# Fourth block's chunk loads issued from GpSimd and sooner, with other PSUM banks, another order of ends, scalings and one last product in a fused retention and MLP kernel

## The chip, the cores and the metric

The kernel runs on one core of a Trainium2 chip. The metric is the device time of one execution in microseconds (us); lower is better. Runs of the kernel before spread from 612.08 to 613.63 us.

## The reference, cut to what matters

Two parts run one after the other: a retention recurrence over 4 batches, 8 heads, 768 tokens and 64 dimensions, and a two-layer MLP over the 3072 tokens that it gives.

```python
for t in range(S):                      # retention, S = 768
    state = gamma * state + einsum('bhd,bhe->bhde', k[:, :, t], v[:, :, t])
    y[:, :, t] = scale * einsum('bhd,bhde->bhe', q[:, :, t], state)
x = y.transpose(0, 2, 1, 3).reshape(3072, 512)
h = x @ w_in                            # 512 -> 2048
g = where(h > 0, h, exp(min(h, 0)) - 1) # ELU
out = g @ w_out                         # 2048 -> 512
```

## The kernel before, in words

**Tiling.** The tokens are cut into 24 chunks of 128 and six blocks of 512 tokens (four chunks each). Block 0 is computed plainly in its first layer; block 1 is computed alone; blocks 2 and 3, and then 4 and 5, are computed as two big blocks of 1024 tokens. Both layers use a seven-product scheme for 2x2 blocks (products numbered 1 to 7, taken in the order 1, 2, 6, 7, 5, 3, 4), nested twice in most stages. A product is a run of matmuls into one PSUM bank; what must be added to it is kept by ScalarE (ACT) copies and VectorE (DVE) sums.

**Order.** The order of instructions on every engine is written out by hand: generators yield at fixed places, and the loop around them calls the next piece of side work. Nothing is rescheduled. An engine runs its own list in order and waits for semaphores.

**PSUM banks.** `bank("a")` has two buffers, `bank("b")` and `bank("d")` one each; `ps_r` (tag "r") has four, shown as `x`, `sc`, `kv`, `y`.

**Retention side work.** For a block, `scores` (L331, masked at L342 on DVE), `states` (L371, summed at L383) and `outputs` (L427, L442) run between the matmuls of the layers. A chunk of q, k, v is one tile of 128x2048 numbers (1 MB) in a pool of four buffers, loaded by `load` (L125) on SP's queue. `scale_v` (L305) multiplies the chunk's v by powers of gamma before `states` may use it, on DVE when `by_vector` is true and on GpSimd (POOL) otherwise. The chunks 8 to 11 belong to block 2, the chunks 12 to 15 to block 3, which the title calls the fourth block.

**Stages that the change touches**, in order of time:

1. About 133 to 190 us: the first layer of block 1, `first(n)` for n = 0 to 3 (matmuls at L784, sums `h` at L731). Its loop loads the chunks 8 to 11, and at n = 3 runs `scores(2, ...)` and the four scalings of these chunks on DVE; then `states(2, ...)` follows.
2. About 183 to 241 us: the second layer of block 1, `second_twice(1, ...)`. Its weights come one product at a time from DRAM into the slots `wq` (L854, 256 KB each, eleven slots, refilled by `fetch` when a product is done), on SP's queue. There are 49 products of eight matmuls (L978). Its inner function `inner(j)` is called for j in `ORDER2 = [1, 2, 6, 7, 5, 3, 4]`. The loop around it loads and scales the chunks 12 to 15 at places of its steps: step n begins with `"first"` and has an `"end"`.
3. About 241 to 296 us: the first layer of the big block (L1279), with `scores(3, ...)` and the rest of block 3's retention.
4. About 296 to 334 us, and again at about 485 to 523 us: the layer of the big block that works with split weights (`passes`, L1342, and `big_rest`, L1329). For n = 0 to 7 it makes `six(n)` and `four(n)`, two sums of passes in PSUM; `six_sum` and `four_sum` (DVE, L918) rescale them and a third pass is added; `begin` (ACT, L1354 and L1355) and `end` (DVE, L1356) make the ELU of C11, C12, C21 and C22. C21 is read from `four`'s bank, C22 from `six`'s.
5. After each of these: the second layer of the big block (L1388), to the end.

The places of the loads and scalings of block 3, before:

```python
LOADS = {(1, "first"): 0, (2, "end"): 1, (4, "end"): 2, (5, "end"): 3}
...
if at in LOADS:
    load(3 * CPB + LOADS[at])
    scale_v(3 * CPB + LOADS[at])
```

Of the kernel before, what the change touches and what calls it, by code (L numbers as in the profile page):

```python
# [28 lines left out]
def kernel(  # L29
# [34 lines left out]
    nc = tc.nc  # L64
# [46 lines left out]
    chunks = [divmod(m, NCH) for m in range(NCHUNK)]  # L111
    raw = {}

    def load(m, cuts=(0, 2048), behind=None):

        if m >= NCHUNK:
            return
        t = ldpool.tile([P, 2048], FP32, name="chunk", tag="chunk")
        raw[m] = (
            t[:, 0:1024].rearrange("p (a h c) -> p a h c", a=2, c=C),  # L120
            t[:, 1024:2048].rearrange("p (a h d) -> p a h d", a=2, d=D),
        )
        hold(t, behind)
        for lo, hi in itertools.pairwise(cuts):
            nc.sync.dma_start(t[:, lo:hi], qkv[m, :, lo:hi])  # L125

    def hold(t, other):

# [697 lines left out]
    def want_second(tb):  # L826

        rest = []
        for j in BIG2 if tb > 1 else ORDER2:
            mine = []  # L830
            for k in (1, 2, 6, 7, 5) + ((4, 3) if j == 4 and tb == NTB - 1 else (3, 4)):
                if k in SMALL:
                    n = SMALL[k]
                    mine.append(((tb, j, k), scratch2[SEVEN[j]][:, 512 * n : 512 * n + 512]))
                else:
                    mine.append(((tb, j, k), scratch[4 * SLOT[j] + {1: 0, 2: 1, 4: 3}[k]].rearrange("p c -> p c")))
            for x in mine[:2] + rest + mine[2:5]:
                want(*x)
            rest = mine[5:]
        for x in rest:  # L840
            want(*x)
# [112 lines left out]
    def second_twice(tb, behind_last):  # L954
        quarter = lambda x, r, t: x[:, 4 * r : 4 * r + 4, P * t : P * t + P]
        ts, kept2 = {}, {}

        def inputs(j):
            for _ in input_parts(j):
                pass  # L960

        def input_parts(j):
            x = gq[INPUT2[j]]
            if j == ORDER2[-1]:
                t = w_all[:, :, 3072:3584].rearrange("p k (f d) -> p k f d", f=4)
            else:
                t = ts_[:, 2 * (len(ts) % 2) : 2 * (len(ts) % 2) + 2].rearrange("p n t -> p (n t)")
                t = t.rearrange("p (k f d) -> p k f d", k=4, f=4)
            b11, b12, b21, b22 = (quarter(x, a, b) for a in range(2) for b in range(2))
            for n, _ in enumerate(quarters_of_input(t, b11, b12, b21, b22)):  # L970
                if n == 1:
                    yield
            ts[j] = {1: b11, 2: b21, 3: b22, 4: t[:, 3], 5: t[:, 0], 6: t[:, 1], 7: t[:, 2]}

        def product(j, k, ps, begin):
            w = where[tb, j, k].rearrange("p (f d) -> p f d", f=4)
            for f in range(4):
                nc.tensor.matmul(  # L978
                    ps, lhsT=w[:, f, :], rhs=ts[j][k][:, f, :], start=(begin and f == 0), stop=(f == 3),
                    skip_group_check=True,  # L980
                )
            done((tb, j, k))

        def copy(ps):
            m = small.tile([P, P], FP32, name="ms", tag="ms")
            nc.scalar.copy(m, ps)
            return m

        def add(o, x, y):
            nc.vector.tensor_tensor(out=o, in0=x, in1=y, op=ALU.add)  # L990

        def inner(j):
            pool, tag = (mpool, "m") if j in (1, 6, 7, 5) else (hpool, "h")
            res = pool.tile([P, 2, 2, P], FP32, name="res", tag=tag)
            pa = bank("a")[:, 0, 0:P]
            product(j, 1, pa, True)
            m1 = copy(pa)
            pb = bank("b")[:, 0, 0:P]
            product(j, 2, pb, True)
            add(res[:, 0, 0], pb, m1)  # L1000
            yield
            product(j, 6, pa, False)
            u2 = copy(pa)
            pd = bank("d")[:, 0, 0:P]
            product(j, 7, pd, True)
            yield
            product(j, 5, pa, False)
            add(res[:, 1, 1], pd, copy(pa))
            yield
            product(j, 3, pa, False)  # L1010
            nc.scalar.copy(res[:, 0, 1], pa)
            yield
            product(j, 4, pd, False)
            add(res[:, 1, 0], pd, u2)
            sum_up(j, res.rearrange("p d t c -> p (d t c)"))

        def store(name, h):
            r, t = int(name[1]) - 1, int(name[2]) - 1
            nc.sync.dma_start(out[tb, r, t].rearrange("p d c -> p (d c)"), h)

        def sum_up(j, m):

            kept2[j] = m
            if j == 2:
                add(m, kept2[1], m)
                store("C11", m)
            elif j == 6:
                add(m, kept2[1], m)
            elif j == 5:
                add(m, kept2[6], m)  # L1030
                h = hpool.tile([P, 512], FP32, name="h", tag="h")
                add(h, m, kept2[7])
                store("C22", h)
                add(kept2[7], kept2[6], kept2[7])
            elif j == 3:
                add(m, kept2[5], m)
                store("C12", m)
            elif j == 4:
                add(m, kept2[7], m)
                store("C21", m)  # L1040

        for _ in input_parts(1):
            yield "input"
        yield "inputs"
        before = iter(())
        for at, j in enumerate(ORDER2):
            cur = inner(j)
            next(cur)
            if j == 1:
                yield "tail"  # L1050
            for _ in before:
                pass
            if at:
                yield "first"
            if j == 2:
                run(changes)
            if j == 7:
                changes = next_input(6)
            if j == 1:

                next(cur)
                yield "elu"
                next(cur)
            parts = input_parts(ORDER2[at + 1]) if at + 1 < 7 else iter(())
            if j in (2, 5, 3):

                next(parts)
            else:
                for _ in parts:
                    pass  # L1070
            if at == 6:
                behind_last()
            if j != 1:
                next(cur)
                yield "middle"
                next(cur)
            for _ in parts:
                pass
            if j == 1:
                flush()  # L1080
                changes = next_input(2)
                some(changes, 3)
            elif j in (7, 5):
                some(changes, 2)
            before = cur
            yield j
        for _ in before:
            yield "rest"
# [629 lines left out]
    for n in range(NQ):  # L1718
# [9 lines left out]
            next(cur)  # L1728
        if n == 3:
            next_part()  # L1730
        next(tail, None)
        next(cur)

# [5 lines left out]
            pass  # L1739
        if n == 3:  # L1740
            retention_step(2, 0)
            scale_v(2 * CPB, True)
        for at, s in enumerate(cur):
            next(sides[n], None)
            next(sides[n], None)
            if n and at >= (1, 2, 1)[n - 1]:
                next_part(n < 3)
            if at == 1 and n == 0:
                some(smalls[2], 2)
            elif at == 1 and n == 3:  # L1750
                for m in range(1, CPB):
                    scale_v(2 * CPB + m, True)
            if s == "gap":
                break
        for _ in sides[n]:
# [35 lines left out]
    flush()  # L1791
    retention_step(2, 2)
    step, VISITS = 0, {(1, "first"): 3, (1, "end"): 4}
    LOADS = {(1, "first"): 0, (2, "end"): 1, (4, "end"): 2, (5, "end"): 3}
    for s in sec:
        if s == "first":
            step += 1
# [7 lines left out]
        if at in VISITS:  # L1805
            retention_step(2, VISITS[at])
        if at in LOADS:
            load(3 * CPB + LOADS[at])
            scale_v(3 * CPB + LOADS[at])
        if at == (4, "end"):  # L1810
            scores(3, 0)
        elif at == (5, "end"):
# [11 lines left out]
    for nb in range(NB):  # L1824
# [3 lines left out]
        any_bank = lambda: ps_r.tile([P, 2, TH], FP32, name="x", tag="r")  # L1828

        def six(m):  # L1830
            q6[m] = any_bank() if m % 4 == 3 else bank("aba"[m % 4])
            passes(nb, m, 6, False, q6[m])

        def six_sum(m):
            stt(q6[m], q6[m], 4097.0, tile_of("C22" if m > 1 else "M1", m), ALU.add)

        def four(m):
            q4[m] = any_bank() if m % 2 else bank("d")
            passes(nb, m, 4, False, q4[m])

        def four_sum(m):
# [115 lines left out]
        for n in range(2 * NQ):  # L1957
# [23 lines left out]
                six_sum(n + 1)  # L1981
            if n == 0:
                end("C11", 2)
                end("C11", 3)
            elif n == 1:
                end("C21", 0)
                end("C11", 6)
            else:
                for x, m in (("C21", n - 1), ("C22", n - 2))[:: 1 if n % 2 else -1]:
                    end(x, m)  # L1990
            if n == 2:
                end("C11", 7)
            if n > 1:
# [108 lines left out]
```

## Time and profile before

| what | value |
|---|---|
| median of three runs | 612.93 us (612.08 to 613.63) |
| the profiled execution, its own time | 612.41 us |
| span of the profiled execution | 610.6 us |
| PE busy | 601.7 us (99%) |
| DVE busy | 507.6 us (83%) |
| ACT busy | 261.9 us (43%) |
| POOL busy | 96.8 us (16%) |
| granted TensorE clock | 1.00 |
| SP's DMA queue | 138.96 MB, 70.7% of 16 engines |
| mean DMA rate over the span | 229 GB/s |

The span is the time from the first to the last instruction on the chip; 1.8 us of the execution lie outside it. PE is TensorE's matmuls, PEld its weight loads, which overlap them. A busy PE is not a PE at its peak, since the ends of matmuls are modelled; so a lost stretch is read best from the distance of the starts of equal work. In the timeline a line gives start, length, engine, source line, operation, tiles, shapes and count, and in brackets the idle time before it and what ended it. In the chain of waits a line gives start, length and the piece of work that was last.

### The profile page before, as it was taken

Reading aid. Unit: us, or ns where it says so; the run is one execution under the profiler, and the core shown is the slowest. Engines: PE = TensorE matmul, PEld = TensorE weight load, DVE = VectorE, ACT = ScalarE, POOL = GpSimd, SP = SyncE. Lnnn points to the kernel's source line nnn. Section 1 sums busy time; section 2 is a strip of 40 time slices with the busy share of each in tenths; the row PEclk is TensorE's granted clock in tenths of the full one; section 3 lists DMA queues with packets and bytes.
Section 4 is the critical chain, followed back from the end, with each engine's and each line's share of the span. In section 5 each row is a group of like instructions: output and inputs, shape, how many; then the busy total and the mean of one; then the engine's idle time right before and its main releaser. Section 6 shows DMA issues by size and latency. Waiting matters only on the chain.

```text
span 610.6 us, 13757 instructions
## 1 busy us (share of the span) xinstructions
PE 601.7 (99%) x5510; PEld 493.7 (81%) x5510; DVE 507.6 (83%) x778; ACT 261.9 (43%) x448; POOL 96.8 (16%) x75
## 2 busy tenths in 40 slices
PE   8999999999999999999999999999999999999997
PEld 6765568888889998888766888888888866788886
DVE  6769889989789876889998877898658999778785
ACT  6889744205553112247688410010136779611110
POOL 2011000000220001000698000110000299000000
PEclk9999999999999999999999999999999999999999
DMA  8698578879977999588977445774555566556552
GB/s 307 283 384 310 169 221 265 239 240 263 355 241 232 297 344 345 181 293 277 365 246 224 120 129 157 268 279 122 183 165 162 168 216 183 168 154 186 153 152 114
DMA packets 85680, 139.85 MB, mean 229 GB/s; under 512 B 6896, under 2 KB 46576, under 8 KB 80880
## 3 DMA queue, kind: packets, MB, share of 16 engines
q1 hardware_dynamic: 85616, 138.96, 70.7%
q8 instruction: 44, 0.72, 0.5%
q14 instruction: 20, 0.16, 0.1%
HBM read 105.12 MB, written 33.82 MB: 228 GB/s over the span
## 4 chain that ended last, share of the span: by engine, by line
PE 90%; DMA 4%; DVE 2%; issue 1%; ACT 1%; SPq 1%; POOL 0%; ACTq 0%; DVEq 0%
PE pa L1388 16%; PE pa L1279 9%; PE pd L1388 8%; PE pd L1279 5%; PE pb L1388 4%; PE pa L557 3%; PE x L647 3%; PE pa L978 3%; PE pa L784 3%; DMA wq<-scratch_dram 3%; PE x L1342 3%; PE pb L1279 2%; PE pa L647 2%; PE y L427 2%; PE y L442 2%; PE pd L1342 2%
## 5 line engine op out<-in xcount | busy, mean ns | idle before, releaser
L1396 ACT COPY ms<-pa 128x256 f32<-128x256 f32 x41 | 15.2, 372 | 106.0 <-PE pa L1388 102.9
L1388 PE MATMUL pa<-gC,wq 128*128 128x256 f32 x240 | 56.8, 382 | 0.0
L1388 PEld LDWEIGHTS pa<-gC,wq 128*128 128x128 f32 x240 | 45.1, 190 | 7.2 <-issue 1.0
L305 POOL TENSOR_TENSOR chunk<-chunk,vf 128x512 f32<-128x512 f32 x15 | 18.7, 1256 | 166.0 <-DMA chunk<-in_qkv_dram 102.9
L1355 ACT ACTIVATE r<-r 128x512 f32<-128x512 f32 x64 | 40.4, 631 | 2.0
L1290 ACT COPY m<-pa 128x512 f32<-128x512 f32 x32 | 18.7, 584 | 36.5 <-PE pa L1279 32.2
L1400 DVE TENSOR_TENSOR res<-pd,ms 128x256 f32<-128x256 f32 x26 | 11.0, 422 | 28.0 <-PE pd L1388 17.5
L1388 PE MATMUL pd<-w_all,wq 128*128 128x256 f32 x120 | 28.4, 379 | 0.0
L1356 DVE SCALAR_TENSOR_TENSOR gC<-r,gC 128x512 f32<-128x512 f32 x24 | 28.1, 1178 | 0.0
L926 POOL TENSOR_TENSOR wp<-wp 128x512 fp32r<-128x512 f32 x6 | 8.4, 1400 | 116.4 <-DMA scratch_dram<-wi 102.7
L1388 PEld LDWEIGHTS pd<-w_all,wq 128*128 128x128 f32 x120 | 22.8, 190 | 3.1
L183 ACT ACTIVATE w_all<-wraw 128x1024 uint32<-128x1024 uint32 (+1 forms) x19 | 19.1, 1008 | 14.2 <-PE x L647 9.9
L1850 POOL TENSOR_TENSOR chunk<-chunk,w_all 128x512 f32<-128x512 f32 x4 | 5.1, 1286 | 126.2 <-ACT w_all L1290 126.2
L1370 DVE TENSOR_TENSOR gC<-w_all,gC 128x1024 f32<-128x1024 f32 x20 | 24.2, 1260 | 0.0
L1388 PE MATMUL pa<-ts,wq 128*128 128x256 f32 x96 | 22.9, 381 | 0.0
L1388 PE MATMUL pa<-w_all,wq 128*128 128x256 f32 x96 | 22.9, 381 | 0.0
L185 ACT ACTIVATE w_all<-wraw 128x1024 fp8e4<-128x1024 f32 (+1 forms) x19 | 22.6, 1189 | 0.6
L1388 PE MATMUL pd<-ts,wq 128*128 128x256 f32 x96 | 22.7, 379 | 0.0
L557 PE MATMUL pa<-xb,w_all 128*128 128x512 f32 x48 | 21.5, 597 | 0.0
L1422 ACT COPY res<-pa 128x256 f32<-128x256 f32 x13 | 4.8, 372 | 38.1 <-PE pa L1388 38.1
L213 DVE CUSTOM_DVE_ANT_0 w_all<-wraw,w_all 128x2048 uint16<-128x2048 uint16 (+1 forms) x19 | 20.1, 1057 | 0.8
L514 ACT ACTIVATE r<-r 128x512 f32<-128x512 f32 x32 | 20.2, 630 | 1.0
(361 smaller groups left out, 1605.5 us busy)
## 6 DMA issues: line engine op xcount, KB each, us to landing
wq<-scratch_dram SPq DMA_DIRECT2D x231, 256.0 KB, 3.4
chunk<-in_qkv_dram SPq DMA_DIRECT2D x22, 1024.0 KB, 7.2
wraw<-in_w_dram SPq DMA_DIRECT2D x15, 1024.0 KB, 6.2
scratch_dram<-wp SPq DMA_DIRECT2D x8, 512.0 KB, 4.4
out_dram<-res SPq DMA_DIRECT2D x7, 512.0 KB, 3.4
scratch_dram<-gT SPq DMA_DIRECT2D x12, 256.0 KB, 4.4
wq<-scratch_dram SPq DMA_DIRECT2D x24, 128.0 KB, 3.2
scratch_dram<-w_all SPq DMA_DIRECT2D x12, 256.0 KB, 3.1
```

Of the source, the lines that this page charges most:

```text
L183: nc.scalar.activation(flat, lo, AF.Copy, scale=2.0**-29)
L185: nc.scalar.activation(top, hi.bitcast(FP32), AF.Copy, scale=2.0**-120, saturate=False)
L213: vec.tensor_tensor(out=flat, in0=c, in1=flat, op=ALU.add)
L514: nc.scalar.activation(e, e, AF.Exp, scale=-1.0)
L557: nc.tensor.matmul(hp, lhsT=w[n][:, fi, j // 2, j % 2, :], rhs=xb[:, j, :], start=(j == 0), stop=(j == 3))
L647: nc.tensor.matmul(X[j][:, d, :], lhsT=w[j][:, d * P : d * P + P], rhs=x[j], start=(n == 0 and d == 0), stop=at_end, skip_group_check=True,)
L1279: nc.tensor.matmul(ps[:, f, :], lhsT=w[:, f, :], rhs=big_xs[j][k], start=(begin and f == 0), stop=True, skip_group_check=True,)
L1342: nc.tensor.matmul(joined(ps), lhsT=where[name][:, c : c + P].bitcast(F32R), rhs=x[:, k], start=(not third and c == 0), stop=(k == 1), ski ...
L1355: nc.scalar.activation(r, r, AF.Exp, scale=-1.0)
L1356: return lambda: nc.vector.scalar_tensor_tensor(g, r, -1.0, h, ALU.add, ALU.max)
L1370: nc.vector.tensor_tensor(out=quarter(to, r, t), in0=quarter(x, r, t), in1=quarter(y, r, t), op=op)
L1388: nc.tensor.matmul(ps, lhsT=w[:, f, :], rhs=ts[j][k][:, f // 2, f % 2, :], start=(begin and f == 0), stop=(f == 3), skip_group_check=True,)
```

## The change

- `load` takes a queue. The loads of the chunks 12 to 15 are issued from GpSimd's queue, at earlier places: (1, "first"), (2, "first"), (3, "end") and (4, "end"). The scaling of a chunk is called one place later than its load, also on GpSimd.
- The four scalings of the chunks 8 to 11 on DVE are called earlier: two within n = 2 of `first`, two at the beginning of n = 3, ahead of the scores.
- In the last `inner(j)` of the second layer of block 1 (j = 4), product 4 comes before product 3, into a bank `b` of its own; its summand u2 takes up `pd` first. The order in which the weights of these two are fetched changes with it.
- In stage 4, `six` uses the banks a, b, a, d in turn (before a, b, a, r), and `four` always one of the four r buffers (before d for even n, r for odd n).
- In stage 4 the ends of C22 and C21 always come in this order (before, in turns), and the end of C11's tile 3 comes one step later.

```diff
-    def load(m, cuts=(0, 2048), behind=None):
+    def load(m, cuts=(0, 2048), behind=None, queue=nc.sync):
...
-            nc.sync.dma_start(t[:, lo:hi], qkv[m, :, lo:hi])
+            queue.dma_start(t[:, lo:hi], qkv[m, :, lo:hi])
...
-            for k in (1, 2, 6, 7, 5) + ((4, 3) if j == 4 and tb == NTB - 1 else (3, 4)):
+            for k in (1, 2, 6, 7, 5) + ((4, 3) if j == 4 and tb in (1, NTB - 1) else (3, 4)):
...
+            if j == ORDER2[-1]:
+                pb = bank("b")[:, 0, 0:P]
+                product(j, 4, pb, True)
+                add(u2, pd, u2)
+                add(res[:, 1, 0], pb, u2)
+                yield
             product(j, 3, pa, False)
             nc.scalar.copy(res[:, 0, 1], pa)
-            yield
-            product(j, 4, pd, False)
-            add(res[:, 1, 0], pd, u2)
+            if j != ORDER2[-1]:
+                yield
+                product(j, 4, pd, False)
+                add(res[:, 1, 0], pd, u2)
...
         if n == 3:
             next_part()
+            for m in range(2, CPB):
+                scale_v(2 * CPB + m, True)
...
             retention_step(2, 0)
-            scale_v(2 * CPB, True)
...
-            elif at == 1 and n == 3:
-                for m in range(1, CPB):
-                    scale_v(2 * CPB + m, True)
+            elif at and n == 2:
+                scale_v(2 * CPB + at - 1, True)
...
-    LOADS = {(1, "first"): 0, (2, "end"): 1, (4, "end"): 2, (5, "end"): 3}
+    LOADS = {(1, "first"): 0, (2, "first"): 1, (3, "end"): 2, (4, "end"): 3, (5, "end"): 4}
...
-            load(3 * CPB + LOADS[at])
-            scale_v(3 * CPB + LOADS[at])
+            n = LOADS[at]
+            if n < CPB:
+                load(3 * CPB + n, queue=nc.gpsimd)
+            if n:
+                scale_v(3 * CPB + n - 1)
...
-            q6[m] = any_bank() if m % 4 == 3 else bank("aba"[m % 4])
+            q6[m] = bank("abad"[m % 4])
...
-            q4[m] = any_bank() if m % 2 else bank("d")
+            q4[m] = any_bank()
...
             if n == 0:
                 end("C11", 2)
-                end("C11", 3)
             elif n == 1:
                 end("C21", 0)
+                end("C11", 3)
                 end("C11", 6)
             else:
-                for x, m in (("C21", n - 1), ("C22", n - 2))[:: 1 if n % 2 else -1]:
-                    end(x, m)
+                end("C22", n - 2)
+                end("C21", n - 1)
```

## The prediction

> **What bounds the kernel now.** I read the page first: busy times, then the slices.
>
> ```profile
> PE 601.7 (99%) x5510; PEld 493.7 (81%) x5510; DVE 507.6 (83%) x778; ACT 261.9 (43%) x448; POOL 96.8 (16%) x75
> PE   8999999999999999999999999999999999999997
> DMA  8698578879977999588977445774555566556552
> ```
>
> PE is the bound from end to end and leaves 8.9 us of its span. Nothing that the change does takes matmuls away, so it can only win places where PE stands, and lose by making new ones. Where it stands is read from the chain of waits. In the second layer of block 1 (window 176 to 262 us):
>
> ```profile
> 210.83 9.84 DMA wq<-scratch_dram
> 220.67 0.14 issue
> 220.81 1.13 PE pd L978 x8
> ...
> 238.00 0.02 issue
> 238.02 0.28 ACT ms L986
> 238.29 0.04 issue
> 238.34 1.16 PE pa L978 x8
> 239.50 0.89 PE pd L978 x8
> ```
>
> PE stood for weights that were under way for 9.84 us, and later for a copy on ACT. An undisturbed product is 0.89. In the layer with split weights the chain and the timeline (PE, DVE) show the period of one step, as the distance of the starts of L1329:
>
> ```profile
> 303.19 1.88 PE L1329 MATMUL pa<-xb,w_all 128*128 128x512 f32 x4
> 308.31 1.88 PE L1329 MATMUL pb<-xb,w_all 128*128 128x512 f32 x4
> 312.81 1.88 PE L1329 MATMUL pa<-xb,w_all 128*128 128x512 f32 x4
> ...
> 301.51 2.97 DVE L1356 SCALAR_TENSOR_TENSOR gC<-r,gC 128x512 f32<-128x512 f32 x2
> 304.41 0.69 DVE L918 SCALAR_TENSOR_TENSOR x<-x,m 128x512 f32<-128x512 f32 x1
> ...
> 314.97 0.69 DVE L1356 SCALAR_TENSOR_TENSOR w_all<-r,pd 128x512 f32<-128x512 f32 x1 [0.17 <-ACT r L1355]
> 315.73 0.30 PEld L1342 LDWEIGHTS pd<-xr,wq 128*128 128x128 f32 x2 [0.54 <-PE pa L1342]
> ```
>
> The periods are 5.12, 4.50, then (next starts 317.68, 322.19, 326.66) 4.87, 4.51, 4.47, with the same work in each. So two steps lose 0.62 and 0.38.
>
> **Scalings of block 2.** Timeline, 180 to 190 us:
>
> ```profile
> 179.98 2.48 DVE L305 TENSOR_TENSOR chunk<-chunk,vf 128x512 f32<-128x512 f32 x4
> 180.80 2.40 PE L371 MATMUL kv<-chunk 64*64 64x64 f32 x112
> 188.92 0.68 DVE L731 TENSOR_TENSOR h<-pd,m 128x512 f32<-128x512 f32 x1
> 189.66 0.97 PEld L978 LDWEIGHTS pd<-ts,wq 128*128 128x128 f32 x8 [0.33 <-DVE h L731]
> ```
>
> The `kv` matmuls go at the pace of the scalings (the chain has 2.01 for such a run at 357.25, here 2.33 to the next product at 183.13) and begin 0.1 late; and DVE's list is so long afterwards that `h` frees `pd` late: the product before starts at 188.47, so 189.36 was due and 189.66 came. That is 0.3 + 0.1 + 0.3 = 0.7 us. The change puts the four L305 (0.62 each, 2.5 in all) among DVE's gaps at 166.07 to 167.10, 168.39 to 169.36 and 173.89 to 174.48, which sum to 2.6; the chunks landed by 164.6. The later two stand ahead of ELU sums, which come up to 0.7 later; the next one that PE needs, `h` at 175.09 to 175.77, has until 177.14. So I take -0.7, from 0 to -0.7.
>
> **Product 4 before product 3.** In between ACT copies `pa`, so the wait at 238.34 is covered by 0.89 of matmuls. Lost before: start to start 236.93 to 238.34 is 1.41 against 0.89, and the product after the stop takes 0.99 instead of 0.89. I take -0.6. DVE gets one 128x128 add more (0.28) before the last, and bank `b` must be read before the next stage's second product, two products later, which is cover of some 1.7 us; without it 0.3 comes back. Range 0 to -0.6.
>
> **Banks and ends of the split-weight layer.** The first loss is `four_sum(1)` behind two ends of C11 on DVE (2.97 us; they take 1.49 each here beside GpSimd's work, 0.68 elsewhere). With one of them moved a step later, the sum starts when ACT's copy is done at 303.07, about 1.4 earlier, and PE needs it 0.62 earlier. The moved end falls in a step in which DVE then runs ahead by as much. The second loss is a matmul that wants bank `d` while the end of C21 reads it (until 315.65). With the four r buffers the reader has three steps more. `six(7)` in `d` needs the end of C22(3), which now comes first in its step, two steps before. The bank changes of `six` hold four steps apart, as before. So both losses go: -1.0, in each of two layers (the second has 5.15 and 4.90 at the same steps): -2.0. Range 0 to -2.0; DVE is busy for nearly all of this stage, so that half of it could reappear one step on.
>
> **The loads.** Off SP's list go four issues (0.4 each), which hold up nothing. What counts is when the bytes move. GpSimd's list is then: load 12, load 13, scale 12, load 14, scale 13, load 15, scale 14, scale 15. It is not paced by PE's steps, only by free buffers and landings: chunk 8's buffer is free at 197.7 (the wait that SP shows for its load), the other three when `outputs` is through at 202.3. So load 12 leaves at 197.7, load 13 at 202.4, load 14 behind scale 12 near 206, load 15 near 210, where they left at 197.7, 209.6, 224.0 and 236.4. An issue from GpSimd has no row here: SP's takes 0.4, GpSimd's own work on a chunk 1.3; either lies in GpSimd's idle time and moves these starts by 1 us at most.
>
> All four megabytes thus fall ahead of the weights that PE waited for at 220.67 (the 32nd product's), where two did. There is little slack for them:
>
> ```profile
> core 0: us, PE busy (x) PEld busy (x) DVE busy (x) ACT busy (x) POOL busy (x), PEclk, DMA share, GB/s
> 198.00:213.00 15.00, 15.00 (x225) 14.74 (x215) 12.40 (x27) 2.12 (x8) 1.04 (x1) 1.00 0.91 299
> 213.00:222.00 9.00, 8.16 (x72) 7.84 (x71) 6.98 (x13) 1.33 (x5) 1.14 (x1) 1.00 1.00 375
> ```
>
> Only 9% of 15 us is idle. By landings: in a backlog a 256 KB transfer follows the one before by 0.65 (206.25, 206.89, 207.55); a chunk adds 2.5 (215.33 to 217.84, 229.17 to 231.69) to 4.1 (201.62 to 205.63, 239.22 to 243.31), 3.28 in the mean. After the landing at 201.62 there stand twelve weights, one output store of the same size and four chunks: 201.62 + 13 x 0.65 + 4 x 3.28 = 223.2. PE wants these weights at 217.78 + 2 x 0.89 = 219.56, so it stands 3.6, plus 0.14 from landing to start. What it lost before goes: starts 217.78, 218.97, 220.81 instead of steps of 0.89, 1.25 us. Net +2.5; with 2.5 a chunk -0.6, with 4.1 +5.8. Some of it may show a few products earlier, not more of it. Later the weights have no chunk beside them, but none was late there.
>
> **Sum.** -0.7 - 0.6 - 2.0 + 2.5 = -0.8. The profiled execution took 612.41 (span 610.6 and 1.8 around it), giving 611.6; it lies 0.5 under the median of the runs, 612.93, from which I forecast 612.1. A change of about 0.3% (1.84 us) is what a measurement of this kernel can tell from none.
>
> **Rivals.** *B, the weights keep their pace.* Two queues share the DMA engines, and the sum above lets the chunks go first. If the two share evenly while both have work, weights land every 1.3 instead of 0.65: the 32nd by 201.62 + 13 x 1.3 = 218.5, before 219.56. Then no stall is left: -3.3 - 1.25 = -4.55, 608.4. For it: chunks are not needed before the scores at 222.8. Against it: a row of a chunk is 8 KB, of a weight 2 KB, so that turns row by row would give the chunk four fifths; no run shows two queues so far. [...]
>
> *C, slower: the chunks take the long price.* At 4.1 a chunk the stall is 7.1 at about 212 to 220 us, net +5.8, and with the gains +2.5: 615.4. It eats the gains from 3.5 a chunk on, and is slower than the bound from 3.9 on. For it: the two chunks that took 4.1 did so with the engines over 0.9 busy; against it, the two that took 2.5 stood in a full queue, as these will.
>
> *D, GpSimd's issues hold DVE.* Ends beside GpSimd's work take 1.34 in the mean against 0.68; were each of the four issues and shifted scalings to cost PE 0.66, it is +2.6 on the forecast, 614.7. Against it: GpSimd's four scalings ran here before without a stop of PE behind them. [...]
>
> **How the numbers follow.** Forecast 0.36, B 0.30, C 0.24, D 0.10. Faster by over 0.3%: B, and the forecast where a chunk adds under 3.0 (0.06): 0.36. Slower: C but for 0.02, D for 0.07, and 0.03 of the forecast where the layer's gain fails: 0.32. Within: 0.32. The forecast's own range is 610.5 to 614.3. With B and C in, 608.2 to 615.8.
>
> **What would show it.** In the profile after: periods of 4.5 at all L1329; no wait of `pa L978` for `ms L986` near 238; `kv` in 2.0 near 180. A wait for `wq` of 2 to 4 us between 210 and 222 is the forecast, none is B, over 5 is C. GpSimd's DMA lines show the issue's length, and DVE sums over 0.7 beside them would be D. The forecast is wrong if load 14 or 15 leaves after 215, or if new waits stand in the split-weight layer.

## The result and the profile after

The changed kernel takes 615.76 us in the median (613.11 to 617.17), the kernel before 612.55 in the runs beside it (610.21 to 614.13). The ratio is 1.0052, 95% interval 1.0034 to 1.007: slower by 3.2 us (2.1 to 4.3). Forecast were 612.1, a gain of 0.8 us, and a chance of 0.32 for slower by over 0.3%. The time lies outside the forecast's own range (610.5 to 614.3). It is just inside the wider one (to 615.8) because that range takes in rival C, and C's mechanism is not what the runs show; so this is luck.

The profiled execution of the changed kernel took 617.17 us (span 615.4), one of its long ones. Its page, beside the lines shown of before:

```profile
PE 603.3 (98%) x5510; PEld 494.0 (80%) x5510; DVE 510.4 (83%) x779; ACT 261.8 (43%) x448; POOL 99.3 (16%) x79
PE   8999999999999899999999999999999999999997
DMA  8698578789977998498976345784555576556552
```

PE leaves 12.1 us of its span where it left 8.9, and one slice has fallen to 8: the fourteenth, from 200 to 215 us. The waits of PE (us in total, times, longest) say for what:

```profile
PE pd L978 <- DMA wq<-scratch_dram: 2.0, 1, 2.0
...
PE x L1349 <- DVE x L918: 1.1, 4, 0.4
PE x L1349 <- DMA wq<-scratch_dram: 0.7, 1, 0.7
...
PE pa L978 <- DMA wq<-scratch_dram: 0.5, 1, 0.5
PE pd L1395 <- PE pa L1395: 0.5, 2, 0.3
PE pb L978 <- DMA wq<-scratch_dram: 0.4, 1, 0.4
```

The same list of the kernel before has for this layer:

```profile
PE pd L978 <- DMA wq<-scratch_dram: 0.7, 1, 0.7
...
PE pa L978 <- ACT ms L986: 0.4, 1, 0.4
```

In the second layer of block 1 (L978) the waits for weights are 2.9 us, where before they were 0.7; the split-weight layer (now L1349) waits four times for `four_sum` (L918) and once for a weight; and a new wait, of `pd` at L1395, stands behind each split-weight layer. The two gains that were forecast ahead of them are there. Timeline (PE and DVE) from 165 to 190 us, and the chain of waits:

```profile
165.89 0.68 DVE L305 TENSOR_TENSOR chunk<-chunk,vf 128x512 f32<-128x512 f32 x1
...
168.19 0.69 DVE L305 TENSOR_TENSOR chunk<-chunk,vf 128x512 f32<-128x512 f32 x1
...
170.48 2.35 DVE L305 TENSOR_TENSOR chunk<-chunk,vf 128x512 f32<-128x512 f32 x2
...
180.57 2.08 PE L371 MATMUL kv<-chunk 64*64 64x64 f32 x112
182.58 1.16 PE L978 MATMUL pa<-gC,wq 128*128 128x128 f32 x8
...
188.87 1.16 PE L978 MATMUL pd<-ts,wq 128*128 128x128 f32 x8
```

```profile
207.69 12.69 DMA wq<-scratch_dram
220.38 0.04 issue
220.42 1.16 PE pb L978 x8
...
237.56 0.89 PE pd L978 x8
238.45 0.89 PE pa L978 x8
239.34 0.89 PE pd L978 x8
```

The scalings run 9 to 14 us earlier and `kv` to the next product takes 2.01 instead of 2.33; near 238 every product follows in 0.89, with no stop for ACT's copy. But a weight that was asked for at 207.69 lands 12.69 us later, and PE stands 0.4 for it. The longest stop, of 2.0, comes before that, for a weight that was asked for at 201.18 and landed at 213.02.

To see where the time went, I cut six profiled executions at the same instructions (us; each is one execution, so that a difference under about 0.5 may be chance):

| stretch | before | changed | changed, second profile | loads only | banks and ends only | best |
|---|---|---|---|---|---|---|
| first L784 of block 1 to first L978 | 49.74 | 49.30 | 49.31 | 49.73 | 50.30 | 49.30 |
| from there to the first L1279 | 57.10 | 60.17 | 60.06 | 60.43 | 56.38 | 55.40 |
| to the first L1329 | 62.96 | 63.16 | 66.10 | 62.16 | 62.64 | 62.32 |
| to the first L1388 | 30.94 | 32.03 | 30.64 | 30.89 | 30.73 | 30.70 |
| to the last matmul | 273.04 | 273.61 | 273.66 | 273.00 | 273.64 | 272.66 |

(Lines by the numbers of before.) The second row, the layer that shares the DMA engines with the loads, carries the loss in both profiles of the changed kernel. The second of them has 3.1 us more in the third row, which come back below.

### The profile page after: what moved, and what is told of

Its sections match the earlier page's. It is cut to its first block, busy times and chain, and to the rows that moved or that the text cites. A ratio compares the mean times of both kernels' runs of the same rounds, so it can differ in the third digit from the quotient of the medians.

```text
span 615.4 us, 13748 instructions
## 1 busy us (share of the span) xinstructions
PE 603.3 (98%) x5510; PEld 494.0 (80%) x5510; DVE 510.4 (83%) x779; ACT 261.8 (43%) x448; POOL 99.3 (16%) x79
## 3 DMA queue, kind: packets, MB, share of 16 engines
q0 software_dynamic: 576, 4.19, 1.8%
## 4 chain that ended last, share of the span: by engine, by line
PE 91%; DMA 5%; DVE 2%; issue 1%; ACT 1%; DVEq 0%; SPq 0%
PE pa L1395 16%; PE pa L1286 9%; PE pd L1395 8%; DMA wq<-scratch_dram 5%; PE pa L784 5%; PE pd L1286 4%; PE pb L1395 4%; PE pa L557 3%; PE x L647 3%; PE x L1349 3%; PE pa L978 3%; PE pb L1286 2%; PE pd L784 2%; PE pa L647 2%; PE kv L371 2%; PE y L427 2%
## 5 line engine op out<-in xcount | busy, mean ns | idle before, releaser
L1395 PE MATMUL pa<-gC,wq 128*128 128x256 f32 x240 | 56.8, 381 | 0.0
L1395 PEld LDWEIGHTS pa<-gC,wq 128*128 128x128 f32 x240 | 45.1, 190 | 7.3 <-issue 1.0
L1362 ACT ACTIVATE r<-r 128x512 f32<-128x512 f32 x64 | 40.4, 631 | 2.0
L1363 DVE SCALAR_TENSOR_TENSOR gC<-r,gC 128x512 f32<-128x512 f32 x24 | 29.8, 1246 | 0.0
L1395 PE MATMUL pd<-w_all,wq 128*128 128x256 f32 x120 | 28.5, 380 | 0.5 <-PE pa L1395 0.5
L1395 PEld LDWEIGHTS pd<-w_all,wq 128*128 128x128 f32 x120 | 22.6, 190 | 4.2 <-issue 1.2
L1349 PE MATMUL x<-xl,wq 128*128 128x512 f32 x64 | 23.6, 454 | 1.1 <-DVE x L918 1.1
L1395 PE MATMUL pa<-ts,wq 128*128 128x256 f32 x96 | 22.9, 381 | 0.0
L1395 PE MATMUL pa<-w_all,wq 128*128 128x256 f32 x96 | 22.9, 381 | 0.0
L1395 PE MATMUL pd<-ts,wq 128*128 128x256 f32 x96 | 22.7, 379 | 0.0
L986 ACT COPY ms<-pa 128x128 f32<-128x128 f32 x21 | 5.6, 266 | 36.7 <-PE pa L978 35.2
```

The lines of the kernel that those rows point to most:

```text
L1349: nc.tensor.matmul(joined(ps), lhsT=where[name][:, c : c + P].bitcast(F32R), rhs=x[:, k], start=(not third and c == 0), stop=(k == 1), ski ...
L1362: nc.scalar.activation(r, r, AF.Exp, scale=-1.0)
L1363: return lambda: nc.vector.scalar_tensor_tensor(g, r, -1.0, h, ALU.add, ALU.max)
L1395: nc.tensor.matmul(ps, lhsT=w[:, f, :], rhs=ts[j][k][:, f // 2, f % 2, :], start=(begin and f == 0), stop=(f == 3), skip_group_check=True,)
```

## The experiments

Theory: the loss is the loads' (**L**), because four chunks overtake the weights. Rival: it is the split-weight layer's (**S**), whose banks and ends shift the wait to other steps. Ratios are against the kernel before, run beside; the us in brackets are the interval times 612.4.

**Each part alone, and all but the loads.** The edits are the hunks of the change taken apart: `e_loads_only` has the queue, LOADS and late `scale_v`; `e_layer_only` these:

```diff
-            q6[m] = any_bank() if m % 4 == 3 else bank("aba"[m % 4])
+            q6[m] = bank("abad"[m % 4])
-            q4[m] = any_bank() if m % 2 else bank("d")
+            q4[m] = any_bank()
...
+                end("C11", 3)      # at n == 1, no more at n == 0
...
+                end("C22", n - 2)
+                end("C21", n - 1)
```

`e_scale_m4` has the early scalings and product 4 before 3; `e_no_loads` is the changed kernel without the hunks of `e_loads_only`.

> Theory L (the loads cost the time): the four megabytes ahead of the weights make PE stand three times between 213 and 221 us as in the profile of the changed kernel (2.2, 0.7 and 0.6 us there), and this part alone is slower than the kernel before by 2.5 to 4.0 us. Rival S (the split-weight layer costs the time, and the loads only seem to, since the stops are made good later): this part alone is within 1 us of the kernel before. The recorded sum has +2.5 for it.

> Theory S (the new banks and ends themselves put four_sum late in other steps): the first split-weight layer loses about 1.5 to 2 us again, with waits of a third pass for x L918, and this part alone is 0.5 to 2 us slower. Rival S' (the loss of 2.1 us seen in the first of these layers came with its place in time, after the loads, or with a late load of weights near 303 us): the banks and ends alone gain 0.4 in each of the two layers and pay 0.4 after each for the bank d of six(7), so that this part is within 0.5 us, or gains as recorded, up to -2.0.

> Both theories: the earlier scalings take 0.7 us out of the stretch from 133 to 190 us and the exchange of products 4 and 3 takes 0.6 us out of 236 to 241 us, as the trace of the changed kernel has them, so that this part alone is 1.3 us faster (0.21%), if no later wait takes it back; a rival in which DVE's list or a late load takes it back has it within 0.5 us.

> Everything of the change but the loads. Theory L: all that the loads cost is gone, -1.3 for scalings and products and between -0.8 and +0.8 for the split-weight layer: 0.5 to 2 us faster than the kernel before, 4 us faster than the changed kernel. Theory S: still slower than before by 0.5 to 2 us.

| kernel | median us | ratio, 95% interval | us |
|---|---|---|---|
| loads only | 615.96 | 1.0052 (1.0031 to 1.0073) | +3.2 (1.9 to 4.5) |
| banks and ends only | 612.30 | 0.9999 (0.998 to 1.0018) | -0.1 (-1.2 to 1.1) |
| scalings and product 4 | 610.82 | 0.997 (0.9955 to 0.9985) | -1.8 (-2.8 to -0.9) |
| all but the loads | 611.29 | 0.9988 (0.9968 to 1.0008) | -0.7 (-2.0 to 0.5) |

The loads alone cost as much as the whole change, and without them it is not slower: L holds, and S does not carry the loss alone. The waits of PE of the kernel with the loads only are of the same kind, in the same layer:

```profile
PE pb L978 <- DMA wq<-scratch_dram: 1.9, 1, 1.9
PE pa L978 <- DMA wq<-scratch_dram: 1.8, 2, 1.5
```

**How many chunks go ahead.** (Products are counted from 0 in the expectations: product 31 is the prediction's 32nd.) Only the loads are changed; the chunks 14 and 15 (then only 15) go back to SP's queue and their old places:

```diff
+            n = LOADS[at]
+            if n < 2:                                    # e_three_early: n < 3
+                load(3 * CPB + n, queue=nc.gpsimd)
+            elif n > 2:                                  # e_three_early: n > 3
+                load(3 * CPB + n - 1)
+            if n:
+                scale_v(3 * CPB + n - 1)
```

> The kernel before, with only the chunks 12 and 13 from GpSimd's queue and sooner; 14 and 15 stay on SP's queue at their old places. Theory of the bytes ahead (the loss is the lateness of the first weight behind the last chunk that overtakes; landings 201.62 + n x 0.65 + chunks x 3.28): product 27, due at 216.0, would have its weights at 201.62 + 9 x 0.65 + 2 x 3.28 = 214.0 and product 31, due at 219.6, at 216.6, so no stop is left in this layer and the 1.2 us of the kernel before go too: 1.2 us faster. Rival, the queue itself (any load from GpSimd beside SP's costs the weights about 0.9 us a chunk): 1.8 us slower.

> The same with the chunks 12, 13 and 14 from GpSimd's queue and sooner, 15 on SP's queue at its old place. Theory of the bytes ahead: product 27 at 217.3 against 216.0, so that 1.4 us are lost and 1.2 are won: within 0.7 us of the kernel before. Rival, the queue itself: about 2.7 us slower. If the cost grows by the same amount with each chunk, both are wrong.

Two early: 611.09, ratio 0.999 (0.9971 to 1.001), -0.6 us (-1.8 to 0.6). Three early: 613.4, 1.0023 (1.0007 to 1.0039), +1.4 us (0.4 to 2.4). Four early, above: +3.2. The rival, a price of each load from GpSimd's queue, had 1.8 and 2.7 for the first two; both lie outside. The theory had 1.2 won for two and "within 0.7" for three; the first lies inside the interval, and of the second the interval covers only its upper end. In the profile with two, no product of this layer waits for a weight, and the stretch takes 56.08 us against 57.10; with three the waits are 0.5 and 0.2; with four 1.5, 1.9 and 0.3. So what counts is what lies ahead in the queues, beyond a point. The gain of 1.2 forecast for two was not seen in full in the median: the stop that it removes is not in every execution of the kernel before (below).

**The size of the rows.** The four loads as in the change, each in four pieces:

```diff
-                load(3 * CPB + n, queue=nc.gpsimd)
+                load(3 * CPB + n, (0, 512, 1024, 1536, 2048), queue=nc.gpsimd)
```

> The loads as in the changed kernel (four from GpSimd's queue, sooner), but each in four pieces of 512 columns, so that a row is 2 KB as a row of the weights is; nothing else is changed against the kernel before. If the engines go from queue to queue row by row (in the profile of the changed kernel the two queues show about as many packets of 8 KB as of 2 KB in a stretch, 82 and 86 from 211 to 213 us), the chunk's share falls from four fifths to a half, weights land every 1.3 us, the 27th by 213.3 and the 31st by 218.5, and the stops go: up to 1.2 us faster. If only the bytes count, it costs 3 to 4 us as before. Three GpSimd issues more for each chunk, of unknown length, may take some of it back.

617.06 us, ratio 1.0074 (1.0057 to 1.0092): +4.5 us (3.5 to 5.6). The premise was wrong in one point: the queue made packets of 4 KB out of rows of 2 KB. From the trace's DMA packets:

| kernel, window | GpSimd's queue | SP's queue | shares of bytes |
|---|---|---|---|
| changed, 211 to 213 us | 86 packets of 8 KB, 704 KB | 73 of 2 KB, 150 KB | 82% and 18% |
| four pieces, 210 to 215 us | 280 packets of 4 KB, 1147 KB | 338 of 2 KB, 692 KB | 62% and 38% |

So in these two windows the engines took 86 packets from one queue and 73 from the other, and 280 and 338, and the weights' share of the bytes was 18% beside packets of 8 KB and 38% beside packets of 4 KB. But the greater share did not help: the 27th landed at 220.21 and the 28th at 222.07, against 220.27 and 221.59 with whole rows. From 213 to 223 us the engines moved 379 to 407 KB a us, no more than with the loads only (380 to 445), and the chunks' bytes were still ahead of the 28th product's weights. Whether packets of 2 KB on both sides would do better stays open; it was not tried.

**Queue and place apart.** The loads at their new places on SP's queue, and at their old places on GpSimd's:

```diff
-                load(3 * CPB + n, queue=nc.gpsimd)
+                load(3 * CPB + n, queue=nc.sync)          # e_loads_sp
...
-            load(3 * CPB + LOADS[at])
+            load(3 * CPB + LOADS[at], queue=nc.gpsimd)    # e_loads_gpold
```

> The loads at the new places and the scalings later, as in the changed kernel, but on SP's queue, in its order and pace; nothing else is changed against the kernel before. Theory of the bytes ahead: SP reaches the places only as its weights are fetched, which is after about 216 us for chunk 14 and 224 for chunk 15, so two or three chunks lie ahead of product 31 and none more: between 1.2 us faster and 1 us slower. Rival, the places cost the time whatever the queue: 3 to 4 us slower.

> The kernel before with the four loads on GpSimd's queue at their old places in the order, so that each is followed by its own scaling. GpSimd is not paced by PE, only by landings: load 13 leaves behind the scaling of chunk 12 near 207 us, load 14 near 216, load 15 near 224. Theory of the bytes ahead: no more than two chunks lie ahead of product 27 and part of a third ahead of 31: within 1 us of the kernel before. Rival, the queue itself: 3 to 4 us slower as in the changed kernel.

SP: 613.15, 1.001 (0.9989 to 1.0031), +0.6 us (-0.7 to 1.9). GpSimd at old places: 612.95, 1.0012 (0.9996 to 1.0028), +0.7 us (-0.2 to 1.7). Neither half alone does the harm. On SP the loads left at 197.27, 207.41, 217.02 and 225.28, paced by the weights before them in the list; on GpSimd at old places at 197.94, 206.57, 215.82 and 226.01, each held by its own scaling. Only both together let the fourth leave at 212.11 (213.50 with the loads only): behind load 13, which waited for PE to leave its buffer, GpSimd's list has nothing in it that follows PE.

**The split-weight layer.** Six(7) goes back to an r buffer; banks and ends are else those of the change:

```diff
-            q6[m] = bank("abad"[m % 4])
+            q6[m] = any_bank() if m == 7 else bank("abad"[m % 4])
```

> The kernel before with the change's banks and ends of the split-weight layer, but six(7) in one of the r buffers, as before, and not in bank d. Theory: the stop of PE in front of the following layer's first product in bank d (two stops of 0.26 and 0.24 us, each with a slower start, 0.48 us of lost time each, in the profile of the banks and ends alone) is the price of six(7) in d and goes; the periods stay at 4.48, 4.50 and 5.15 in the first three steps against 5.12, 4.50 and 4.87 before, 0.35 less in each layer: 0.7 us faster. Rival: DVE's list, not the bank, ends last there, and the 0.48 stay or move.

612.2 us, ratio 1.0014 (0.9996 to 1.0033): +0.9 us (-0.2 to 2.0), where 0.7 less was expected; the runs do not show a gain. The profile shows what was meant: the stop behind the layer is gone. Timeline (PE) with banks and ends only, its periods and this stop:

```profile
302.75 1.88 PE L1329 MATMUL pa<-xb,w_all 128*128 128x512 f32 x4
...
307.23 1.88 PE L1329 MATMUL pb<-xb,w_all 128*128 128x512 f32 x4
...
311.73 1.88 PE L1329 MATMUL pa<-xb,w_all 128*128 128x512 f32 x4
313.85 0.73 PE L1342 MATMUL x<-xl,wq 128*128 128x512 f32 x2 [0.24 <-DVE x L918]
...
316.89 0.59 PE L1329 MATMUL pd<-xb,w_all 128*128 128x512 f32 x1
...
339.08 1.10 PE L1388 MATMUL pd<-w_all,wq 128*128 128x256 f32 x4 [0.26 <-PE pa L1388]
```

and with six(7) in an r buffer:

```profile
336.07 1.89 PE L1388 MATMUL pa<-gC,wq 128*128 128x256 f32 x8
337.79 1.89 PE L1388 MATMUL pd<-w_all,wq 128*128 128x256 f32 x8
```

There `pd` follows `pa` in 1.72, as one product follows the other. What DVE still reads in bank d is the sum of C12 and the end of C22 that six(7) leaves: in the kernel with banks and ends only, its last end with `pd` runs from 338.14 to 338.82. Each such stop with its slow start is 0.48 (the last row of the first table holds both, less the 0.35 won in the second of these layers: 0.60).

**Which version is best.** The scalings, product 4, and only two chunks early (`e_best0`); the same with banks, ends and six(7) in an r buffer (`e_best`).

> The kernel before with the change's scalings and order of products 4 and 3, and only the chunks 12 and 13 from GpSimd's queue and sooner; no change in the split-weight layer. Theory: the parts add up, -1.6 and about -1.0, 2.6 us faster than the kernel before, and faster than the changed kernel by 6. Rival: the weights' chain of refills takes back what the earlier PE wins, and it is no better than the scalings and products alone (1.6).

> The same with the banks and ends of the split-weight layer and six(7) in an r buffer. If the parts add up, 0.7 us less than the version without: 3.3 us faster than the kernel before. If the layer gives nothing, the same as that version within 0.5 us.

610.2, ratio 0.9969 (0.9953 to 0.9986), -1.9 us (-2.9 to -0.9), where 2.6 were expected; and 609.27, 0.9961 (0.9945 to 0.9978), -2.4 us (-3.4 to -1.3), where 3.3 were expected if the parts add up. Both beat the kernel before and the changed one. They are not told apart from each other, nor from the scalings and product 4 alone (-1.8).

**Why the whole is worse than its parts.** The parts alone add up to 3.2 - 0.1 - 1.8 = 1.3 us, the whole has 3.2. The three intervals together leave about 2 us of doubt in the first figure, so that this difference alone is not clear of noise. Three runs: the changed kernel again, the same without banks and ends, and the same with the chunks 14 and 15 back on SP.

```diff
+            q6[m] = any_bank() if m % 4 == 3 else bank("aba"[m % 4])   # e_no_layer: as before
...
+            elif n > 2:                                               # e_after_two: as in two early
+                load(3 * CPB + n - 1)
```

> The changed kernel once more, for a second profiled execution. If the three waits for four_sum in the first split-weight layer (2.1 us more than before in the first profile) belong to the change, they are here again; if that execution was a chance one, the first three periods are 4.48, 4.50 and 5.1 and the rest 4.5, as with the banks and ends alone. The median stays at 615 to 616 us either way.

> The changed kernel without its banks and ends in the split-weight layer (loads, scalings and product order stay). If the layer's part costs 2 us in this company: 613 to 614 us, 1 to 1.5 us slower than the kernel before. If it costs next to nothing (2 x 0.48 paid, 2 x 0.35 won): 0.3 us below the changed kernel, 2.5 to 3 us slower than the kernel before.

> The changed kernel with only the chunks 14 and 15 put back to SP's queue at their old places; all else of the change stays. Theory of the bytes ahead: the stops for weights between 213 and 221 us go and with them the whole loss: 1.5 to 2.5 us faster than the kernel before, 4 to 5 us faster than the changed kernel. Rival, part of the loss is the split-weight layer's: within 1 us of the kernel before.

Changed again: 615.98, 1.0059 (1.0037 to 1.0081), +3.6 us (2.3 to 5.0). Without banks and ends: 614.3, 1.0029 (1.0015 to 1.0043), +1.8 us (0.9 to 2.6). With 14 and 15 back: 612.39, 1.0006 (0.9986 to 1.0025), +0.4 us (-0.9 to 1.5), within 1 us of before, as the rival of that run had it. So in this company the loads of 14 and 15 cost about 3.2 us, and banks and ends about 1.8, with some 1.6 of doubt, where banks and ends alone cost nothing that could be seen. The profiles show two things that add to the stops; that they make up the whole of the 1.8 is not shown.

First, GpSimd. In the first profile of the changed kernel and in the one with 14 and 15 back, PE stands 0.72 and 0.55 for a weight at the entry of the split-weight layer; then the third, fifth and sixth period are longer (5.34, 5.09, 4.24, and 5.44, 5.07, 4.25, against 5.16, 4.48 and 3.59 with banks and ends only). Timeline of the changed kernel (PE, DVE, POOL):

```profile
324.71 1.88 PE L1336 MATMUL pa<-xb,w_all 128*128 128x512 f32 x4
326.78 0.73 PE L1349 MATMUL x<-xl,wq 128*128 128x512 f32 x2 [0.20 <-DVE x L918]
...
323.17 0.68 DVE L1855 TENSOR_TENSOR gC<-pd,gC 128x512 f32<-128x512 f32 x1
323.77 2.35 DVE L1363 SCALAR_TENSOR_TENSOR gC<-r,gC 128x512 f32<-128x512 f32 x1
326.04 0.69 DVE L918 SCALAR_TENSOR_TENSOR x<-x,m 128x512 f32<-128x512 f32 x1
...
323.18 2.39 POOL L945 TENSOR_TENSOR gC<-gC,gC 128x1024 f32<-128x1024 f32 x1
```

An end with both inputs in SBUF takes 2.35 instead of 0.68: it is over at 326.12, 0.55 behind the end of GpSimd's operation (323.18 + 2.39 = 325.57), as if it had begun only then. `four_sum` behind it is late. The ends of 1.16, 1.40 and 2.25 at 315.38, 319.46 and 329.03 are likewise over 0.55 to 0.56 behind the end of an operation of GpSimd's (315.99, 320.30 and 330.73); what holds them back was not tried apart. In the second profile of the changed kernel the stop at the entry is 1.78 us instead, and the periods are 4.98, 4.74 and 3.57: the price of a stop was not the same in the two. That other ends then meet GpSimd's operations is my reading of these numbers and was not measured. The expectation that the pattern comes again, or goes, was too simple.

The other profiles show that such a stop costs more with the new banks and ends than with the old. Timeline (PE) of the entry with two early, which has the old ones, and with 14 and 15 back:

```profile
299.53 0.74 PE L1342 MATMUL x<-xr,wq 128*128 128x512 f32 x2 [0.62 <-DMA wq<-scratch_dram]
```

```profile
298.00 0.73 PE L1349 MATMUL x<-xr,wq 128*128 128x512 f32 x2 [0.55 <-DMA wq<-scratch_dram]
```

Five profiles with the old banks (two early, three early, loads on SP, GpSimd at old places, scalings and product 4) have a stop of 0.20 to 0.94 there. Their first period is 4.47 to 4.66 instead of 5.12, which fits a PE that comes later to a `four_sum` that is ready, and the layer (fourth row of the first table) takes 29.91 to 30.50. Without a stop it takes 30.6 to 30.9 with the old and 30.7 with the new banks. The three with the new banks and such a stop take 32.22, 32.03 and 30.64. So the 0.62 that the change was to win here is not lost in every execution of the old order either: a stop ahead of the layer takes its place.

Second, the clock. In the chain of waits without banks and ends, three products behind the stop take 1.64, 1.71 and 1.20 instead of 0.89:

```profile
208.29 12.94 DMA wq<-scratch_dram
221.23 0.14 issue
221.37 1.64 PE pa L978 x8
223.00 1.71 PE pd L978 x8
224.71 1.20 PE pa L978 x8
225.91 0.89 PE pd L978 x8
```

The view by windows shows the granted clock there (the columns are those of the prediction's windows; the clock is the third from the end):

```profile
222.00:223.00 1.00, 1.00 (x6) 1.00 (x6) 0.00 (x0) 0.00 (x0) 0.00 (x0) 0.50 1.04 381
223.00:224.00 1.00, 1.00 (x7) 1.00 (x6) 0.00 (x0) 0.27 (x1) 0.00 (x0) 0.50 1.03 381
```

Six matmuls a us instead of twelve, for some 3 us, and 1.9 us lost in these three products, of which about 0.25 is the slow start that a product has behind a stop anyway (1.13 to 1.16). In the record of the clock the half lasts 3.41 us each time: from 221.82 here; from 214.38 in the first profile of the changed kernel, where part of it hides behind the next late weight; and in the second from 219.32 and again from 304.66, behind the stop of 1.78 at the entry of the split-weight layer. A mean clock below 0.9985 was granted in 19 of the 48 executions of kernels with all four chunks early on GpSimd's queue, and in 7 of the 123 executions of the kernel before beside the experiments. By (1 - mean clock) x 612 that is 0.7 to 1.2 us an execution in these (five sets of executions) against 0.1 to 0.3 before. What brings the half on is not shown: in the first profile of the changed kernel it begins 1.2 us behind a stop of 2.05 and at the beginning of one of 0.52 (214.27 to 214.79), and in the profile with the loads only stops of 1.95 and 0.25 had none behind them (clock 1.00 from 198 to 226 us).

## Why the prediction was wrong, by its steps

The forecast missed by 4.0 us (-0.8 against +3.2). By the parts measured alone, the gain of banks and ends that did not come is 1.9 of it, the loads are 0.7, and scalings and product 4 gave 0.5 more than forecast; the 1.9 left appear only when the parts are together.

- **Scalings, -0.7, and product 4, -0.6: right.** `kv` to the next product is 0.32 shorter, the 0.3 of `pd` behind `h` is gone (188.87 follows without a wait), and the last four products of the layer take 3.57 instead of 4.19 up to the next layer in all eight profiles with the new order. Alone they give -1.8 (-2.8 to -0.9), and the forecast of -1.3 lies in it.
- **Banks and ends, -2.0: this step failed.** "So both losses go" was said of each layer's 0.62 and 0.38. The first went: 5.12 became 4.48. The second did not: 4.87 became 5.16. The prediction had named new waits in this layer as a sign of being wrong. The bank was freed, but PE now comes 0.64 earlier to a sum that does not come earlier: the L918 that PE waits for in this step is done 11.05 us after the layer's first L1329 (302.75 to 313.80), and was done 11.02 after it before (303.19 to 314.21). DVE's list, with an end of 1.17 ahead of it in both, sets this step. The sum had priced each wait alone, and the prediction's own reserve ("half of it could reappear one step on") was what happened; but the sum took the full 2.0. So 0.35 is won in each layer. And a cost had no term: six(7) takes bank d into the next layer, 0.48 twice. Net +0.26 by the profile, -0.1 (-1.2 to 1.1) measured alone, +1.8 in company.
- **Loads, +2.5: right in sign and place, too small.** Alone they cost 3.2 (1.9 to 4.5). The landings were as worked out: the last of the twelve weights (the 32nd product's, number 31) was put at 223.2 and landed at 223.07 in the first profile, at 223.62 with the loads only, and at 221.34 and 223.28 in the second profile and without banks and ends. The interval holds 2.5 too; that it was too small is read from the profile with the loads only, where 43.04 us pass from the first L978 to the scores, 4.7 more than the 38.38 that the profile before has without its 1.25, and the sum had 3.74. What failed is "not more of it" for the products ahead: lateness was taken at the product that waited before, and it is greatest at the first weights behind the last chunk. Weights land every 0.65 and PE uses one in 0.89, so that from there on each product wins back 0.24 of slack in the queue, but PE has already stood. By the same formula product 28 gives 201.62 + 10 x 0.65 + 4 x 3.28 = 221.24 against 216.89, which is 4.5 us of stop with the 0.14 to its start; minus 1.25 it is 3.2. With the loads only it landed at 221.59, 0.2 behind chunk 15.
- **The 1.25 that goes was no constant.** With the same loads as before, the stretch from the first L978 to the scores takes 39.63 in the profile before, but 38.98, 39.03, 38.81 and 38.60 in four others: against the 38.38 without the 1.25 that is a stop of 0.2 to 1.25, which depends on how the transfers fall. Some 0.6 could be won on average, not 1.25, so that the loads looked cheaper than they are: 4.5 - 0.6 would be 3.9, which the interval holds as well.
- **Beyond the sum**: the half clock behind the stops (0.50 for 3.41 us), and the longer ends beside GpSimd's operations (2.35 and 2.25 instead of 0.68). Nothing in the profile of before shows the first; it was not among the unknowns.
- **The rivals.** B fell: PE does wait for weights, and giving them more of the engines (38% of the bytes instead of 18%) did not help. C named the time (615.4) but not the cause: its price of 4.1 a chunk would put the 32nd weight at 201.62 + 13 x 0.65 + 4 x 4.1 = 226.5, 3 us later than it landed. D fell: GpSimd's four issues take 0.73, 0.53, 0.59 and 0.59 us, and no wait of PE follows from them. GpSimd's list left as forecast at first (197.22 and 201.89 for 197.7 and 202.4; 206.51 and 212.11 for 206 and 210).

What stays open: whether the split-weight layer's 1.8 us in company are all due to GpSimd's alignment and the clock, since the two profiles of the changed kernel differ there by as much (32.03 and 30.64, and 63.16 and 66.10 ahead of it). Bank d of six(7) is a rival that one pair of runs speaks for: the best version and the changed kernel with 14 and 15 back differ in nothing but the bank of six(7), and are 2.8 us apart (about 1.2 to 4.3). Two stops of 0.48 account for 1.0 of it; the first has no stop at the entry in its profile, and the second has one of 0.55. Against it, with banks and ends only the r buffer was not better (+0.9 against -0.1, with intervals that overlap).

## What to carry to other kernels

When transfers overtake others, work out the lateness at the first transfer behind the last overtaker, not at the one that was late before; and ask what paces the new queue, since a list that holds nothing of the slow engine's work can run ahead by itself (here the fourth load left at 212.11 from GpSimd's list and at 225.28 from SP's). Before you sum up waits that end, shift the whole schedule by the first and look whether the next one's producer is early enough. A stop that one profile shows is worth what several executions show of it.

## What the runs showed of the hardware that was not expected

- A granted clock of 0.50 for 3.41 us, from 214.38, from 221.82, and from 219.32 and 304.66, in three of the five profiles with four chunks early on GpSimd's queue, each time close behind stops of PE for weights. The other two had such stops as well, and a clock of 1.00 from 198 to 226 us.
- Loads from GpSimd's queue with rows of 2 KB made packets of 4 KB (1280 packets for four chunks against 576 with rows of 8 KB, the small ones that end a transfer among them).
- Shares of the bytes of two queues: 82% to 18% with packets of 8 KB against 2 KB (211 to 213 us, changed kernel), 62% to 38% with 4 KB against 2 KB (210 to 215 us, four pieces). The weights of 256 KB that the changed kernel asked for from 199.40 to 207.69 took 8.2 to 12.7 us to land, against a median of 3.4 over the whole kernel.
